# Attention and two MLPs on one core: the first four units' probabilities turned by a product with diagonals of reciprocals

## The chip, the cores and the metric

The kernel runs on one core of one Trainium2 chip. A core has TensorE (PE in the profile, its weight loads PEld), VectorE (DVE), ScalarE (ACT), GpSimd (POOL) and SyncE (SP, which here issues nearly all DMAs). The metric is device time in microseconds. The kernel before took 1039.23 us (median of three runs, 1036.81 to 1042.94).

## The reference

Inputs are q, k, v of shape (4, 8, 576, 64), s of shape (4, 8, 576), and two pairs of MLP weights, 512 x 2048 and 2048 x 512 in 64-bit floats.

```python
scores = scale * np.matmul(q, k.transpose(0, 1, 3, 2))
cum = np.cumsum(np.maximum(s, 0.0), axis=-1)
bias = -(cum[:, :, :, None] - cum[:, :, None, :])
scores = np.where(causal, -1e9, scores + np.minimum(bias, 0.0))
attn = np.exp(scores - max(scores))
attn = attn / (sum(attn) + 1e-09)
x = (attn @ v)                         # to 2304 x 512
x = (s1 * relu(x @ w_in1)**2 + b1) @ w_out1
h = x @ w_in2
out = (relu(h) + alpha * min(h, 0)) @ w_out2
```

## The kernel before, in words

Attention is cut into 32 units: a batch, a pair of heads, and a range of query rows. `units` (L272) lists them so that the first four units (n = 0 to 3) are batch 0, rows 0 to 319, its four pairs of heads. Each unit has two heads (h = 0, 1), and a head of these units has three blocks of query rows (`IB`, L52: 64, 128 and 128 rows).

For a head `scores` (L402) first writes the bias into the tile `probs`, from a running sum that a DMA has spread over the partitions (`u.cums`): on VectorE for head 0 (L433), on ScalarE for head 1 (L429). GpSimd masks it (L437). TensorE makes scores (L455), VectorE joins both and takes the maximum (L459), ScalarE takes the exponential and its row sums (L471). Then VectorE adds 1e-9 to the sums (L478) and takes their reciprocals (L479), and GpSimd multiplies each block of probabilities by them (L482, three instructions for a head of units 0 to 3).

`values` (L488) turns the probabilities on TensorE against `ident` (L513: six transposes of 128 x 128 for such a head, five into one PSUM bank and one into another). The banks are copied to SBUF by ScalarE and VectorE (L517), multiplied with v (L529), and copied into the rows of x (L544). `busy` (L94) issues products of a tile of zeros that nobody reads, on TensorE, in the first four units.

The running sums are made once (`sum_gates`, L109), written to `cum_d` in DRAM, and read back by `load_cum` (L345), two DMAs for a unit, each spread over 128 partitions. `load_qk` and `load_v` load q, k and v. `fetch(0, f)` (L189) loads packet f of the first MLP's weights, two DMAs of 512 KB, and `packet(0, f)` turns it into pairs of 32-bit tiles: ScalarE L140 and L130, VectorE L141, L142 and L131, GpSimd L131 for half of it. The order of these loads at the start is written out in `attention` (L565 to L586). Tiles of units 1 to 3 lie in slots of the weights to come, which `early_bufs` hands out in the order of the calls.

The first MLP block starts when all four units of batch 0, rows 0 to 319, are in x (`while done < reached(0)`, L978). Behind that TensorE works through 128-row products of the two MLPs with the other attention units in between (`pace`, L965). The order in which the instructions stand in each engine's queue is planned ahead for the whole program, from the order of the program text and from modelled costs; on the chip each engine then takes its queue strictly in that order, and a wait holds all that stands behind it.

The slopes of the second MLP (`nalpha`) are loaded by `load_constants` in the opening (L104, a DMA of single elements of 4 bytes, and L105 on VectorE); they are first read in the second MLP (L826), from 642.7 us on.

Of the kernel before, what the change touches and what calls it, by code (L numbers as in the profile page):

```python
# [8 lines left out]
F32 = mybir.dt.float32  # L9
# [4 lines left out]
ALU = mybir.AluOpType  # L14
# [5 lines left out]
def tile_forget_attention__then__two_mlps(  # L20
# [20 lines left out]
    nc = tc.nc  # L41
    B, H, S, D = q.shape
    NT, DM = out.shape
    DFF = w_in1.shape[1] // 2
    P = 128
    NP = H // 2
    NCC = DM // P
    NF = DFF // P
# [3 lines left out]
    IB = [(0, 64)] + [(64 + 128 * n, 192 + 128 * n) for n in range(4)]  # L52
    R1 = IB[2][1]
    QK = S - R1 + S
    EARLY, NATIVE = NP, 2 * NP

# [3 lines left out]
    REBASE, W_SCALE = 2.0**-111, 2.0**8  # L62
# [4 lines left out]
    one = ctx.enter_context(tc.tile_pool(name="one", bufs=1))  # L67
# [33 lines left out]
    def load_constants():  # L101
        nc.sync.dma_start(out=gate_s, in_=act_s.partition_broadcast(P))
        nc.sync.dma_start(out=gate_b, in_=act_b.partition_broadcast(P))
        nc.sync.dma_start(out=nalpha, in_=alpha.rearrange("(f p) -> p f", p=P))  # L104
        nc.vector.tensor_scalar(out=nalpha, in0=nalpha, scalar1=-1.0, scalar2=None, op0=ALU.mult)  # L105
        nc.vector.tensor_scalar(out=gate_s, in0=gate_s, scalar1=1.0 / W_SCALE, scalar2=None, op0=ALU.mult)
        nc.vector.tensor_scalar(out=gate_b, in0=gate_b, scalar1=1.0 / W_SCALE, scalar2=None, op0=ALU.mult)

    def sum_gates(first):  # L109

# [165 lines left out]
    class Unit:  # L276
        def __init__(self, n):
            self.n = n
            self.b, self.pr, self.rng = units[n]
            self.tag = "_".join(str(i) for i in units[n])  # L280
            self.h0 = 2 * self.pr
            self.blocks = (0, 1, 2) if self.rng == 0 else (3, 4)
            self.q0, self.q1 = (0, R1) if self.rng == 0 else (R1, S)
            self.nv = 3 if self.rng == 0 else 4
            self.probs = [None, None]

            self.early = 0 < n < EARLY
            self.native = n < NATIVE
            self.n_banks = 0
            self.cums = []  # L290

# [53 lines left out]
    def load_cum(u, heads=(0, 1)):  # L345
        for h in heads:
            cr = u.buf(two, S, F32, "cum", f"cum{h}")
            (nc.sync if u.n else nc.scalar).dma_start(
                out=cr[:, : u.q1], in_=cum_d[u.b * H + u.h0 + h, : u.q1].partition_broadcast(P)
            )  # L350
            u.cums.append(cr)
# [50 lines left out]
    def scores(u, h):  # L402
# [11 lines left out]
        for r in u.blocks:  # L414
            i0, i1 = IB[r]
            rows = i1 - i0
            if u.early and r != 1:
                big, col = u.buf(two, 0, F32, "", f"probs{h}{r}"), 0

            width = -(-i1 // P) * P if i1 < S else S  # L420
            pt = probs[r] = big[:, col : col + width]
            col += width
            if width > i1:
                nc.gpsimd.memset(pt[:, i1:], 0.0)
            if r == 0:
                nc.gpsimd.memset(pt[64:P, 0:64], 0.0)

            if flip:
                nc.scalar.activation(  # L429
                    pt[:rows, :i1], u.cums[h][:rows, :i1], AF.Relu, scale=-1.0, bias=cumT[:rows, r, head : head + 1]  # L430
                )
            else:
                nc.vector.tensor_scalar(  # L433
                    out=pt[:rows, :i1], in0=u.cums[h][:rows, :i1], scalar1=cumT[:rows, r, head : head + 1],
                    scalar2=0.0, op0=ALU.subtract, op1=ALU.min,
                )
            nc.gpsimd.affine_select(  # L437
                out=pt[:rows, i0:i1], in_=pt[:rows, i0:i1], pattern=[[-1, rows]], base=0,
                channel_multiplier=1, compare_op=ALU.is_ge,
                fill=-MASKED if flip else MASKED,  # L440
            )
# [35 lines left out]
            busy(4)  # L477
        nc.vector.tensor_scalar(out=sm[:, :nr], in0=sm[:, :nr], scalar1=1e-9, scalar2=None, op0=ALU.add)  # L478
        nc.vector.reciprocal(sm[:, :nr], sm[:, :nr])  # L479
        for m, r in enumerate(u.blocks):  # L480
            rows, n = IB[r][1] - IB[r][0], IB[r][1]
            nc.gpsimd.tensor_scalar(  # L482
                out=probs[r][:rows, :n], in0=probs[r][:rows, :n], scalar1=sm[:rows, m : m + 1],
                scalar2=1.0, op0=ALU.mult, op1=ALU.mult,
            )
        yield

    def values(u, h):  # L488
# [10 lines left out]
        for n_bank, bank in enumerate(banks):  # L499
            f0, fn = bank[0][1], bank[-1][1] + width[bank[-1][0]]  # L500
            tp = u.bank("tr", f"pt{h}_{n_bank}")
            moves = []
            for c, off in bank:
                for r in u.blocks:
                    i0, i1 = IB[r]
                    if P * c >= i1:
                        continue

                    partial = r and P * c > i0
                    o = off + i0 - max(q0, P * c)  # L510
                    moves.append((not partial, -c if partial else o, o, r, min(P * c, S - P)))
            for _, _, o, r, k0 in sorted(moves):
                nc.tensor.transpose(tp[:, o : o + P], u.probs[h][r][:, k0 : k0 + P], ident)  # L513
            n_p = (2 * h + n_bank) % 2
            if u.native:
                pf = two.tile([P, 512], F32, tag=("ph", "pl")[n_p], name=f"pf_{u.tag}_{h}_{n_bank}")
                (nc.scalar.copy, nc.vector.tensor_copy)[n_p](pf[:, f0:fn], tp[:, f0:fn])  # L517
                parts = (pf,)
            else:
                ph = two.tile([P, 512], F32R, tag="ph", name=f"ph_{u.tag}_{h}_{n_bank}")  # L520
                pl = two.tile([P, 512], F32R, tag="pl", name=f"pl_{u.tag}_{h}_{n_bank}")
                split(ph[:, f0:fn], pl[:, f0:fn], tp[:, f0:fn])
                parts = (ph, pl)
            yield
            for z, part in enumerate(parts):
                for c, o in bank:
                    w = width[c]
                    lhs = (u.vn if u.native else u.vs[h])[:, c].rearrange("p z d -> p (z d)")
                    nc.tensor.matmul(  # L529
                        av[:, nq - w : nq], lhs, part[:, o : o + w],  # L530
                        start=(c == 0 and z == 0), stop=(c == last_c and z == len(parts) - 1),
                        skip_group_check=True,
                    )
# [28 lines left out]
    def attention():  # L562
# [5 lines left out]
        load_qk(us[2])  # L568
        load_v(us[0])
        load_cum(us[1])  # L570
        fetch(0, 0)
        load_qk(us[3])
        load_cum(us[2])
        load_v(us[1])
        packet(0, 0)
        load_cum(us[3])
        fetch(0, 1)
        load_v(us[2])
        load_v(us[3])
# [13 lines left out]
        u = Unit(EARLY)  # L593
# [391 lines left out]
    for n in range(len(BLOCKS) * NF):  # L985
# [13 lines left out]
            lent.clear()  # L999
        if n == NF - 2:  # L1000
            sum_columns()
        if len(late) > LAG[layer]:
            step(*late.pop(0))

# [49 lines left out]
```

## Time and profile before

| | |
|---|---|
| median of three runs | 1039.23 us |
| profiled execution, its own time | 1039.36 us |
| its span (first to last instruction) | 1037.6 us |
| around the span | 1.8 us |
| PE busy | 1018.5 us (98%) |
| PEld busy | 925.5 us (89%) |
| DVE busy | 674.4 us (65%) |
| ACT busy | 670.7 us (65%) |
| POOL busy | 450.6 us (43%) |
| mean granted TensorE clock | 0.996 |

Busy time is what an engine spent in instructions; matmuls are pipelined and their ends are modelled, so a busy TensorE isn't one at its peak, and the share of weight loads (PEld) says more on that. A row of the timeline has start, duration, engine, line, operation, output and input, shape and count, and in brackets the idle time before it and what ended it. Rows with a count join several instructions and name the first one's shape. The granted clock is a share of 2.4 GHz.

### The profile page before, as it was taken

What the parts mean: (1) busy time and instruction counts of PE and PEld (TensorE: products, weight loads), DVE (VectorE), ACT (ScalarE), POOL (GpSimd) and SP (SyncE); (2) the same over time, 40 slices, a digit from 0 to 9 for tenths busy, and PEclk for the clock granted to TensorE, in tenths of its full rate; (3) what the DMA queues carried; (4) which work ended last, traced back from release to release, by engine and by line L of the source; (5) the groups of instructions that cost most, each with busy time, mean ns of one, the idle gap of its engine ahead of it and who ended that gap; (6) DMA issues with size and microseconds to landing.
All of it is one profiled execution on the core that took longest, in us unless ns stands there. A gap on an engine that the chain in (4) does not pass through costs nothing. (4 is left out here: it accounts for less than half of the span.)

```text
span 1037.6 us, 20643 instructions
## 1 busy us (share of the span) xinstructions
PE 1018.5 (98%) x6949; PEld 925.5 (89%) x6952; DVE 674.4 (65%) x1605; ACT 670.7 (65%) x1668; POOL 450.6 (43%) x876
## 2 busy tenths in 40 slices
PE   9999999999999999999999999999999999999997
PEld 4578899999999999999999888888999999999996
DVE  6899665687677766677655865857665456455443
ACT  5878766777787877878776776645554454445433
POOL 5555675666677576777562000574611011001000
PEclk9899999999999999999999999999999999999999
DMA  7997443343143432324215762645644335334331
GB/s 150 257 249 223 120 76 68 73 98 76 40 89 67 99 72 52 82 65 91 68 34 177 230 199 78 205 148 176 200 154 142 102 114 171 103 102 133 105 102 48
DMA packets 197930, 125.45 MB, mean 121 GB/s; under 512 B 138496, under 2 KB 167936, under 8 KB 197824
## 3 DMA queue, kind: packets, MB, share of 16 engines
q1 hardware_dynamic: 193744, 123.56, 42.8%
q8 instruction: 55, 0.90, 0.4%
q10 hardware_dynamic: 4080, 0.57, 0.3%
q14 instruction: 51, 0.42, 0.1%
HBM read 106.19 MB, written 17.90 MB: 120 GB/s over the span
## 5 line engine op out<-in xcount | busy, mean ns | idle before, releaser
L781 PE MATMUL hp<-xh,w 128*128 128x256 f32 (+1 forms) x1024 | 229.9, 301 | 1.1 <-ACT r L800 1.1
L905 PE MATMUL acc<-w,ring 128*128 128x512 f32 x864 | 214.6, 392 | 1.1 <-DVE ring L131 0.7
L905 PEld LDWEIGHTS acc<-w,ring 128*128 128x128 f32 x864 | 155.9, 188 | 29.4 <-DVE ring L131 1.1
L781 PEld LDWEIGHTS hp<-xh,w 128*128 128x128 f32 x1024 | 171.4, 189 | 9.3 <-ACT r L800 1.4
L895 PE MATMUL acc<-gh,w 128*128 128x256 f32 x896 | 170.3, 286 | 0.4 <-ACT res L924 0.4
L781 PE MATMUL hp<-xl,w 128*128 128x256 f32 (+1 forms) x512 | 152.3, 298 | 0.0
L895 PEld LDWEIGHTS acc<-gh,w 128*128 128x128 f32 x896 | 135.3, 189 | 2.4 <-ACT res L924 1.0
L881 POOL TENSOR_TENSOR cc<-u,t 128x256 f32<-128x256 f32 x32 | 26.9, 839 | 237.2 <-DVE u L872 202.9
L895 PE MATMUL acc<-gl,w 128*128 128x256 f32 x448 | 117.7, 288 | 1.4 <-POOL gl L131 1.4
L482 POOL TENSOR_SCALAR probs<-probs,sm 64x64 f32<-64x64 f32 (+4 forms) x160 | 89.2, 571 | 58.9 <-DVE sm L479 51.9
L471 ACT ACTIVATE probs<-probs,nm 64x64 f32<-64x64 f32 (+4 forms) x160 | 89.9, 562 | 35.8 <-DVE nm L459 26.9
L131 POOL TENSOR_TENSOR gl<-r,gh 128x256 fp32r<-128x256 f32 x112 | 87.7, 784 | 51.3 <-ACT gh L130 41.4
L815 PE MATMUL p<-xs,sums 128*128 128x256 f32 x768 | 104.6, 282 | 0.4 <-DVE u L857 0.4
L815 PEld LDWEIGHTS p<-xs,sums 128*128 128x128 f32 x768 | 98.0, 189 | 2.0 <-DVE u L857 0.6
L781 PEld LDWEIGHTS hp<-xl,w 128*128 128x128 f32 x512 | 97.1, 190 | 2.7
L459 DVE CUSTOM_DVE_ANT_0 probs<-sc,probs 128x320 f32<-128x320 f32 (+3 forms) x160 | 68.4, 428 | 42.1 <-PE sc L458 28.8
L815 PEld LDWEIGHTS p<-xs,w 128*128 128x128 f32 x576 | 79.0, 189 | 8.4 <-DVE u L872 1.7
L800 ACT ACTIVATE r<-hp 128x256 f32<-128x256 f32 (+1 forms) x144 | 58.0, 403 | 43.7 <-PE hp L781 31.6
L815 PE MATMUL p<-xs,w 128*128 128x256 f32 x576 | 82.0, 282 | 2.3 <-DVE u L872 1.5
L895 PEld LDWEIGHTS acc<-gl,w 128*128 128x128 f32 x448 | 79.8, 189 | 2.5 <-POOL gl L131 1.9
L513 PE MATMUL pt<-ident,probs 128*128 128x128 f32 x480 | 75.3, 275 | 3.1 <-POOL probs L482 2.7
L826 DVE SCALAR_TENSOR_TENSOR ph<-pl,misc,ph 128x512 f32<-128x512 f32 x64 | 50.6, 790 | 42.3 <-ACT pl L842 42.3
(151 smaller groups left out, 2104.3 us busy)
## 6 DMA issues: line engine op xcount, KB each, us to landing
sums<-sums_d SPq DMA_DIRECT2D x128, 256.0 KB, 2.7
wi<-in_moe_w_in_dram SPq DMA_DIRECT2D x32, 512.0 KB, 5.0
wo<-in_moe_w_out_dram SPq DMA_DIRECT2D x32, 512.0 KB, 5.1
cum<-cum_d SPq DMA_DIRECT2D x32, 288.0 KB, 3.6
sums_d<-w SPq DMA_DIRECT2D x64, 128.0 KB, 1.9
cum<-cum_d SPq DMA_DIRECT2D x30, 160.0 KB, 3.0
nat<-in_k_dram SPq DMA_DIRECT2D x64, 72.0 KB, 2.5
x_d<-res SPq DMA_DIRECT2D x18, 256.0 KB, 2.4
```

The source lines that it names most:

```text
L131: lo_eng.tensor_tensor(out=lo, in0=src, in1=hi.bitcast(F32), op=ALU.subtract)
L459: nc.vector.tensor_tensor_reduce(out=pt[:rows, j0:j1], in0=scr, in1=pt[:rows, j0:j1], scale=SCALE if flip else -SCALE, scalar=init, op0=AL ...
L471: nc.scalar.activation(pt[:rows, :n], pt[:rows, :n], AF.Exp, bias=nm[:rows, m : m + 1], scale=1.0 if flip else -1.0, accum_out=sm[:rows, m ...
L482: nc.gpsimd.tensor_scalar(out=probs[r][:rows, :n], in0=probs[r][:rows, :n], scalar1=sm[:rows, m : m + 1], scalar2=1.0, op0=ALU.mult, op1=A ...
L513: nc.tensor.transpose(tp[:, o : o + P], u.probs[h][r][:, k0 : k0 + P], ident)
L781: nc.tensor.matmul(hs, a[:, c], b[c], start=(n == 0), stop=(n == len(terms) * NCC - 1))
L800: relus.append(nc.scalar.activation(r, hs, AF.Relu, scale=1.0 / W_SCALE).ins)
L815: nc.tensor.matmul(bank, lhs[:, c * P : (c + 1) * P], rhs[:, c], start=(start and c == 0 and z == 0), stop=(c == 1 and z == 2), skip_group ...
L826: nc.vector.scalar_tensor_tensor(out=r, in0=u, scalar=nalpha[:, f : f + 1], in1=r, op0=ALU.mult, op1=ALU.add).ins
L881: nc.gpsimd.tensor_tensor(out=cc[:, T:], in0=u3, in1=t5, op=ALU.add)
L895: nc.tensor.matmul(banks[d] if count == 2 else acc[d // 2][:, d % 2], a[:, d * P : (d + 1) * P], b, start=(f == 0 and (d % 2 == 0 or count ...
L905: nc.tensor.matmul(banks[m], a[:, m * P : (m + 1) * P], b, start=(f == 0 and b is woh and a is gh), stop=(f == NF - 1 and a is gl),)
```

## The change

For units 0 to 3 (`SPREAD = 4`) GpSimd no longer multiplies the probabilities by the reciprocals. VectorE writes three diagonal matrices for a head (identity times reciprocal: 64 x 64, 128 x 128, 128 x 128) into a tile that shares its place with `xs0` or `xs1`, one place for each h; and the six transposes of a head become six ordinary 32-bit products with these diagonals, 64 or 128 columns wide, so that turning and scaling are one step. The zeroing of a quarter of the first block's tile (L426) falls away for these units.

The running sums of units 2 and 3 are asked for right behind those of unit 1, ahead of the first packet of weights. The slopes of the second MLP are loaded at the start of the third block of the first MLP (`n == 2 * NF`) and no longer in the opening.

```diff
-    EARLY, NATIVE = NP, 2 * NP
+    EARLY, NATIVE, SPREAD = NP, 2 * NP, 4
...
     def load_constants():
         nc.sync.dma_start(out=gate_s, in_=act_s.partition_broadcast(P))
         nc.sync.dma_start(out=gate_b, in_=act_b.partition_broadcast(P))
+        nc.vector.tensor_scalar(out=gate_s, in0=gate_s, scalar1=1.0 / W_SCALE, scalar2=None, op0=ALU.mult)
+        nc.vector.tensor_scalar(out=gate_b, in0=gate_b, scalar1=1.0 / W_SCALE, scalar2=None, op0=ALU.mult)
+
+    def load_slopes():
         nc.sync.dma_start(out=nalpha, in_=alpha.rearrange("(f p) -> p f", p=P))
         nc.vector.tensor_scalar(out=nalpha, in0=nalpha, scalar1=-1.0, scalar2=None, op0=ALU.mult)
-        nc.vector.tensor_scalar(out=gate_s, in0=gate_s, scalar1=1.0 / W_SCALE, scalar2=None, op0=ALU.mult)
-        nc.vector.tensor_scalar(out=gate_b, in0=gate_b, scalar1=1.0 / W_SCALE, scalar2=None, op0=ALU.mult)
...
+            self.spread = n < SPREAD
+            self.diag = [None, None]
...
-            if r == 0:
+            if r == 0 and not u.spread:
                 nc.gpsimd.memset(pt[64:P, 0:64], 0.0)
...
         nc.vector.reciprocal(sm[:, :nr], sm[:, :nr])
+        if u.spread:
+            u.diag[h] = one.tile([P, QK], F32, tag=f"xs{h}", name=f"diag{h}_{u.tag}")
         for m, r in enumerate(u.blocks):
             rows, n = IB[r][1] - IB[r][0], IB[r][1]
+            if u.spread:
+                turn = u.diag[h][:rows, m * P : m * P + rows]
+                nc.vector.tensor_scalar(
+                    out=turn, in0=ident[:rows, :rows], scalar1=sm[:rows, m : m + 1], scalar2=None, op0=ALU.mult
+                )
+                continue
             nc.gpsimd.tensor_scalar(
...
-                    moves.append((not partial, -c if partial else o, o, r, min(P * c, S - P)))
-            for _, _, o, r, k0 in sorted(moves):
+                    moves.append((not partial, -c if partial else o, o, r, min(P * c, S - P), max(0, P * c - i0)))
+            for _, _, o, r, k0, skip in sorted(moves):
+                if u.spread:
+                    rows = IB[r][1] - IB[r][0]
+                    at = (r - u.blocks[0]) * P
+                    nc.tensor.matmul(
+                        tp[:, o + skip : o + rows], u.probs[h][r][:rows, k0 : k0 + P],
+                        u.diag[h][:rows, at + skip : at + rows], start=True, stop=True,
+                    )
+                    continue
                 nc.tensor.transpose(tp[:, o : o + P], u.probs[h][r][:, k0 : k0 + P], ident)
...
         load_cum(us[1])
+        load_cum(us[2])
+        load_cum(us[3])
         fetch(0, 0)
         load_qk(us[3])
-        load_cum(us[2])
         load_v(us[1])
         packet(0, 0)
-        load_cum(us[3])
         fetch(0, 1)
...
+        if n == 2 * NF:
+            load_slopes()
```

## Rows read from the trace of the kernel before

**Rows 1.** Busy time of each engine by stretch, with granted clock and DMA share.
```profile
core 0: us, PE busy (x) PEld busy (x) DVE busy (x) ACT busy (x) POOL busy (x), PEclk, DMA share, GB/s
15.00:30.00 15.00, 13.72 (x61) 7.63 (x61) 11.62 (x45) 9.80 (x31) 9.68 (x29) 1.00 0.78 207
30.00:45.00 15.00, 13.70 (x53) 8.31 (x53) 11.85 (x47) 14.14 (x42) 5.84 (x14) 0.77 0.92 240
...
100.00:110.00 10.00, 10.00 (x66) 8.47 (x65) 9.98 (x22) 9.47 (x23) 7.48 (x12) 1.00 0.62 168
...
300.00:400.00 100.00, 100.00 (x836) 99.76 (x835) 71.36 (x207) 78.53 (x210) 67.91 (x141) 1.00 0.35 77
```

**Rows 2.** Idle time by what ended it, first 66 us: total us, times, longest.
```profile
PEld pt L513 <- POOL probs L482: 5.1, 8, 1.4
ACT probs L429 <- DMA cum<-cum_d: 4.5, 3, 2.0
...
DVE pf L517 <- PE pt L513: 2.7, 2, 1.3
...
DVE wt L141 <- ACT wt L140: 1.9, 2, 1.2
```

**Rows 3.** Groups by line and shape, first 60 us: GpSimd's multiplications.
```profile
L482 POOL TENSOR_SCALAR probs<-probs,sm 128x320 f32<-128x320 f32 x8 | 4.7, 588 | 0.0
...
L482 POOL TENSOR_SCALAR probs<-probs,sm 128x192 f32<-128x192 f32 x8 | 4.0, 495 | 0.0
...
L482 POOL TENSOR_SCALAR probs<-probs,sm 64x64 f32<-64x64 f32 x8 | 3.0, 381 | 14.0 <-DVE sm L479 7.9 <-DVE nm L468 5.9 <-DVE pf L517 0.2
```

**Rows 4.** Timeline of VectorE in the opening.
```profile
13.76 0.98 DVE L433 TENSOR_SCALAR probs<-cum,cumT 64x64 f32<-64x64 f32 x3 [0.61 <-DMA cum<-cum_d]
...
22.79 1.65 DVE L433 TENSOR_SCALAR probs<-cum,cumT 64x64 f32<-64x64 f32 x3
...
26.10 2.69 DVE L433 TENSOR_SCALAR probs<-cum,cumT 64x64 f32<-64x64 f32 x3
...
36.17 0.91 DVE L141 TENSOR_SCALAR wt<-wt 128x512 uint32<-128x512 uint32 x1
...
39.82 0.42 DVE L141 TENSOR_SCALAR wt<-wt 128x512 uint32<-128x512 uint32 x1
...
41.62 0.17 DVE L105 TENSOR_SCALAR misc<-misc 128x16 f32<-128x16 f32 x1
...
41.84 0.40 DVE L131 TENSOR_TENSOR xl<-xf,xh 128x256 fp32r<-128x256 f32 x1
...
48.06 0.68 DVE L131 TENSOR_TENSOR xl<-xf,xh 128x256 fp32r<-128x256 f32 x1
...
53.03 1.14 DVE L131 TENSOR_TENSOR xl<-xf,xh 128x256 fp32r<-128x256 f32 x1
```

**Rows 5.** Timeline of GpSimd: the half of a weight packet.
```profile
27.35 1.26 POOL L131 TENSOR_TENSOR w<-wt,w 128x512 fp32r<-128x512 f32 x1
```

**Rows 6.** Timeline of TensorE: one head's transposes, one head's products with v.
```profile
15.90 0.82 PE L513 MATMUL pt<-ident,probs 128*128 128x128 f32 x6
...
18.91 1.30 PE L529 MATMUL acc_first<-pf,vn 128*128 128x320 f32 x6
```

**Rows 7.** Timeline of SyncE: the running sums of units 2 and 3.
```profile
19.41 0.93 SPq L348 DMA_DIRECT2D cum<-cum_d  x2
...
21.39 0.96 SPq L348 DMA_DIRECT2D cum<-cum_d  x2
```

**Rows 8.** Busy time by stretch, single microseconds around the lower clock; columns as Rows 1.
```profile
33.00:34.00 1.00, 0.70 (x5) 0.50 (x6) 0.86 (x2) 0.97 (x5) 0.94 (x3) 1.00 0.96 353
...
36.00:37.00 1.00, 0.65 (x3) 0.50 (x3) 1.00 (x3) 1.00 (x5) 0.94 (x4) 0.57 0.99 320
...
42.00:43.00 1.00, 1.00 (x4) 0.38 (x2) 0.23 (x1) 0.97 (x3) 0.98 (x3) 0.52 1.09 416
```

## The prediction
> **What bounds the kernel now.** I read busy time by stretch first. Late in the kernel TensorE is the bound without doubt: from 300 to 400 us it is busy for 100.00 us of 100 and its weight loads for 99.76. In the opening it is not: its weight loads fill 7.63 of 15 us (15 to 30) and 8.31 of 15 (30 to 45), and much of what it does there is products of zeros. The fullest queues there are VectorE's, 11.62 and 11.85 of 15, with ScalarE's at 14.14 in the second of the two. VectorE stays full long into the first MLP block, 9.98 of 10 us from 100 to 110, with TensorE's weight loads at 8.47 [rows 1]. So the change, which touches the first 60 us and one small load later, is priced along VectorE's queue: what leaves it, what enters it, and which of its waits go. A microsecond won there is taken as one won at the end, because TensorE has no idle time behind.
>
> The view of waits says what the opening waits for: the weight loads of the transposes stood 5.1 us in all for GpSimd's multiplications (8 times), ScalarE 4.5 us for running sums that had not landed (3 times), VectorE 2.7 us for turned probabilities (twice) and 1.9 us for ScalarE's step of a weight packet (twice) [rows 2].
>
> **Part 1a: GpSimd's multiplications go.** Their three shapes took 4.7, 4.0 and 3.0 us, 11.7 us in all for the eight heads [rows 3]. GpSimd isn't the bound, so this is worth nothing by itself. It is worth something where an instruction of VectorE ran beside one and was longer for it. In VectorE's timeline I look for equal instructions with and without a multiplication beside them: a bias of three blocks took 1.65 us against 0.98; a 512-column shift 0.91 against 0.42 (two such); two low halves of x 0.68 and 1.14 against 0.40 [rows 4]. The excess is 0.67 + 2 x 0.49 + 0.28 + 0.74 = 2.7 us. Taken: -2.7. Bounds: 0, if GpSimd's other work moves into the same places, and -2.7.
>
> **Part 1b: VectorE gets 24 diagonals.** No row shows a 128 x 128 of this kind. The nearest are the same operation from SBUF to SBUF on 16 columns, 0.17 us, and on 512 columns, 0.42 us [rows 4]; between them 0.5 ns a column, so 0.19 us for 64 columns and 0.23 us for 128, 0.65 us for a head, 5.2 us for eight. Below, 24 x 0.17 = 4.1 us; above, a diagonal may meet a GpSimd instruction, which is a rival below. Not all of it is on the path: VectorE is idle for 3.4 + 3.15 = 6.5 us between 15 and 45 us [rows 1], of which 1.9 us goes by part 2, so 4.6 us of holes remain, some of them right behind a reciprocal, where it waits for the turned block. I let these hide 2.0 us. Taken: +3.2; bounds 0.6 (all holes used) and 5.2.
>
> **Part 1c: transposes become products.** A head's six transposes take 0.82 us. Six 32-bit products of 64 or 128 columns are two passes each, 2 x 576 = 1152 columns in all, which is just what a head's products with v have: 1.30 us [rows 6]. So TensorE gets 8 x 0.48 = 3.8 us more; the 12 weight loads in place of 6 could make it 6 to 8 us. Against that stand its waits for GpSimd, 5.1 us [rows 2], which shrink to the wait for one diagonal, some 0.3 us a head, 2.4 us. The time from reciprocal to turned block stays about as it was. Taken: 0, bounds -2.7 and +4. What hides it is VectorE's longer queue; without that cover it costs 3.8 us.
>
> **The clock.** From 36 to 43 us the granted clock is 0.57, then 0.50, then 0.52, the 1.2 GHz level (seven rows, first and last shown). Ahead of the fall TensorE had holes: busy 0.70 of the microsecond from 33, behind a wait for GpSimd [rows 8]. The level lasted some 6.1 us, 3 us of TensorE's time at full speed. With those waits shorter and more work in their place I expect less of it, hardly surely. On VectorE's queue it is worth one wait for turned probabilities, 1.3 us, the longer of the two [rows 2]. Taken: -1.3; bounds -3.0 and 0 (the lower clock stays, or comes elsewhere).
>
> **Part 2: running sums of units 2 and 3 earlier.** SyncE issued them at 19.41 and 21.39 us [rows 7]; right behind unit 1's they go out some 9 us earlier. ScalarE's two long waits for them, 3.9 of the 4.5 us, should go; on VectorE they came through as the 1.9 us in which it waited for ScalarE's step of a packet [rows 2]. Taken: -1.9; bounds -3.9 and 0. Moved behind them are the first packet of weights, unit 3's q and k and unit 1's v, each by two issues of 0.93 and 0.96 us [rows 7] and the 640 KB that they move. The first packet is used when the first MLP block starts, 35 us after it was ready, which hides 2 to 3 us. If ScalarE's first step on it stands in the queue ahead of an exponential, it costs up to those 3 us; I take 0.
>
> **Part 3: the slopes later.** One VectorE instruction of 0.17 us [rows 4] and one small DMA leave the opening; 200 us on, they meet a VectorE that is busy 71% of the time from 300 to 400 us [rows 1] and values not read before the second MLP. Taken: -0.2. If the load is slow to land, what stands behind the sign change on VectorE waits, at most for some microseconds, with TensorE's queue still full ahead of it; taken 0, above +2.
>
> **The sum.** -2.7 + 3.2 + 0 - 1.3 - 1.9 - 0.2 = -2.9 us. The profiled execution took 1039.36 us (span 1037.6 and 1.8 around it), 0.13 us over the median of the runs. 1039.36 - 2.9 = 1036.5 us. What a measurement here can tell from no change is about 0.5%, 5.2 us, so the likeliest case is no change by that measure.
>
> **Rivals.**
>
> Rival A, the opening hangs on TensorE more than on VectorE. For it: its waits for GpSimd are the longest of those that the change aims at, and the slow clock lies behind them. Against it: half of its work there is zeros. Then 5.1 (waits) + 3.0 (clock) + 1.9 (sums) - 3.8 (longer products) = 6.2 us go: 1033.1 us. It needs the lower clock to go wholly.
>
> Rival B, slower: the diagonals meet GpSimd's other instructions. The place is VectorE's queue between 27 and 50 us, beside the low halves of weight packets on GpSimd, 1.26 us each [rows 5]. The row of three biases at 26.10 us took 2.69 us in place of 0.98, beside that very instruction [rows 4]: 1.7 us lost. Then the diagonals cost their full 5.2 us, 4 of the 8 heads lose 1.26 us each, 5.0 us, nothing is won by 1a (GpSimd's weight halves move up into the places that came free), and the lower clock stays: 5.2 + 5.0 - 1.9 - 0.2 = +8.1, 1047.5 us. With two heads caught it is already +5.6. Against it: such blocks hit three or four instructions of VectorE now, among over a hundred. The Trainium skill, page "SBUF — State Buffer", section "Who interferes with whom", puts it as an exclusive lock: whichever of a VectorE instruction of this kind and a GpSimd instruction starts first has the shared ports for the whole instruction, and the other is fully blocked. By that rule a diagonal could lose a whole GpSimd instruction, and the rows just named agree with it, 2.69 against 0.98 us.
>
> Rival C, only VectorE's total counts. VectorE is full until 110 us [rows 1], and the opening's shorter waits only make it wait in the first MLP block for weights. Then +5.2 - 2.7 - 0.2 = +2.3 us: 1041.7 us.
>
> Rival D, the change does not do all it says: the order in the queues is planned for the whole program, and the moved sums, planned as landing in time either way, may stay where ScalarE waits. Then the sum lacks 1.9: 1038.4 us.
>
> **Chances.** The forecast 0.35, rival A 0.30, B 0.13, C 0.15, D 0.07. Faster by over 0.5% (under 1034.0) is most of A and a little of the forecast's own spread, 0.31; slower by over 0.5% (over 1044.6) is B and a little of C, 0.14; the rest, 0.55, lies within. The range runs from 1031.0 (A with the bound of 3.9 for the sums) to 1043.5 (C with up to 2 us of the slopes' load); below and above I leave 0.1 each. The likeliest case's own range is 1034 to 1039.
>
> **What would show it.** Right: ScalarE's waits for running sums down to that of unit 1; no excess on VectorE beside a multiplication; diagonals of about 0.2 us; six products of a head in 1.2 to 1.8 us; the first product of the MLP, now at 58.7 us, some 3 us earlier, and the rest of the kernel moved by as much. Wrong: diagonals of 1 us or more (B); the first MLP block starting earlier but ending no earlier (C); the granted clock never under 1.00 in the opening and a start more than 5 us earlier (A).

## The result: 0.9% slower, and the profile after

The changed kernel took 1048.3 us (median of six runs, 1043.36 to 1051.23) against 1038.83 for the kernel before (six runs, 1036.81 to 1042.94): ratio 1.0086, 95% interval 1.0066 to 1.0106. That is 9.5 us slower; 1036.5 was forecast, and 1048.3 lies over the top of the range. The profiled execution took 1047.07 us, its span is 1045.3 us and its mean granted clock 0.991 (before 1037.6 us and 0.996). In all that follows, a run that took over 1.5% more than the fastest of its kernel is left out of medians and ratios: three runs of e18 and one of the kernel before.

The page of the kernel after: busy time of TensorE, and its clock in 40 slices of 26 us.

```profile
PE 1030.1 (99%) x7000; PEld 936.2 (90%) x7000; DVE 670.3 (64%) x1629; ACT 673.6 (64%) x1668; POOL 438.9 (42%) x844
...
PEclk9699999999999999999999999999999999999999
```

TensorE is busy for 11.6 us more than before, more than the whole loss, and the second slice is the only one with a low clock. So the loss lies in the opening. Busy time by stretch of the kernel after, to be held against [rows 1]; the last row is the stretch at the 1.2 GHz level:

```profile
15.00:30.00 15.00, 14.27 (x73) 9.47 (x72) 10.25 (x48) 9.91 (x32) 5.67 (x22) 1.00 0.89 224
30.00:45.00 15.00, 13.23 (x44) 8.75 (x43) 11.03 (x40) 11.30 (x31) 3.23 (x6) 0.63 0.80 221
...
34.00:51.00 17.00, 16.98 (x49) 11.67 (x50) 10.26 (x38) 10.39 (x30) 2.58 (x4) 0.50 0.81 205
```

VectorE, the queue by which everything was priced, is now less busy in the opening than before, and TensorE is busy for 16.98 us of the 17 at the low clock. Who waits for whom has turned round. The view of waits of the kernel after, first 66 us, for ScalarE and VectorE:

```profile
ACT pf L537 <- PE pt L528: 8.6, 6, 3.3
ACT wt L142 <- DMA wi<-in_moe_w_in_dram: 1.5, 1, 1.5
ACT wt L142 <- DMA wo<-in_moe_w_out_dram: 1.2, 1, 1.2
...
DVE probs L463 <- PE sc L459: 7.3, 7, 2.2
DVE pf L537 <- PE pt L528: 4.0, 4, 1.5
DVE wt L143 <- ACT wt L142: 2.5, 2, 1.9
...
DVE turnedq L377 <- DMA natq<-in_q_dram: 0.4, 1, 0.4
```

The waits at which the change aimed are gone: none of ScalarE's for running sums and none of TensorE's for GpSimd's multiplications is left of [rows 2]. In their place ScalarE (8.6 us) and VectorE (7.3 and 4.0 us) wait for TensorE, and three loads are waited for that were not in the kernel before: the two of the second weight packet, and unit 3's q. VectorE's wait for ScalarE's step of a packet, which was to go, grew from 1.9 to 2.5 us.

What these waits lead to is seen in the timeline of the kernel after. First TensorE with a head's products at 2.4 GHz (12 instructions: each 32-bit product is two), then its two holes and products at 1.2 GHz; then SyncE's issues, ScalarE and VectorE ahead of the second hole.

```profile
16.54 1.78 PE L528 MATMUL pt<-diag,probs 128*128 128x64 f32 x12
23.56 1.80 PE L528 MATMUL pt<-diag,probs 128*128 128x64 f32 x12 [0.73 <-DVE diag L490]
34.02 1.00 PE L459 MATMUL sc<-turnedk,turnedq 64*128 64x192 f32 x2 [1.76 <-DVE nm L463]
38.42 2.72 PE L528 MATMUL pt<-diag,probs 128*128 128x64 f32 x10
...
9.94 2.81 SPq L352 DMA_DIRECT2D cum<-cum_d  x6
13.82 3.21 SPq L329 DMA_DIRECT2D natq<-in_q_dram  x4
17.08 4.90 SPq L329 DMA_DIRECT2D natk<-in_k_dram  x4
23.06 0.49 SPq L210 DMA_DIRECT2D wi<-in_moe_w_in_dram  x1
...
27.82 0.68 ACT L142 ACTIVATE wt<-wi 128x512 f32<-128x512 f32 x1 [1.48 <-DMA wi<-in_moe_w_in_dram]
30.22 0.67 ACT L142 ACTIVATE wt<-wo 128x512 f32<-128x512 f32 x1 [1.22 <-DMA wo<-in_moe_w_out_dram]
...
22.46 0.51 DVE L377 STREAM_TRANSPOSE turnedq<-natq 128x320 f32<-128x320 f32 x1 [0.41 <-DMA natq<-in_q_dram]
30.92 0.43 DVE L143 TENSOR_SCALAR wt<-wt 128x512 uint32<-128x512 uint32 x1 [1.91 <-ACT wt L142]
33.61 0.35 DVE L463 CUSTOM_DVE_ANT_0 probs<-sc,probs 128x192 f32<-128x192 f32 x1
```

Read from below: TensorE stood 1.76 us for a maximum of VectorE's, which stood behind weight work that had waited 1.91 us for ScalarE, which had waited 1.48 and 1.22 us for the second packet, issued from 23 us on. Behind that hole the granted clock is 0.50 for 17 us. The first product of the MLP starts at 71.99 us, before at 58.68 us; not all of these 13.3 us are lost, since more of the attention is done by then.

The second packet itself hardly moved. The kernel before issued it at 22.39 us, 0.67 us sooner, and ScalarE came to it only at 29.93 us, behind its waits for running sums, and found it there (SyncE and ScalarE of the kernel before):

```profile
22.39 0.44 SPq L208 DMA_DIRECT2D wi<-in_moe_w_in_dram  x1
29.93 0.67 ACT L140 ACTIVATE wt<-wi 128x512 f32<-128x512 f32 x1
```

Freed from those 3.9 us, ScalarE is there at 26.3 us in the kernel after, and stands 2.7 us for the packet instead.

**Where the time went.** The span is TensorE's idle time, plus what the low clock cost (busy time times one minus the granted clock, summed over stretches of 1 us), plus the rest, called its work at full clock. The work is worked out as this rest, so the three add up to the span in every row, whatever the cause:

| profiled execution | span | idle | lost to clock | work |
|---|---|---|---|---|
| before | 1037.6 | 19.1 | 3.3 | 1015.2 |
| after | 1045.3 | 15.2 | 8.5 | 1021.6 |

So work grew by 6.4 us, the clock cost 5.3 us more, and 3.9 us of holes went: 6.4 + 5.3 - 3.9 = 7.8 us, against 7.7 between the spans.

### The profile page after: what moved, and what is told of

It reads as the page before. It is cut to its first block, busy times and chain, and to the rows that moved or that the text cites. A ratio compares the mean times of both kernels' runs of the same rounds, so it can differ in the third digit from the quotient of the medians.

```text
span 1045.3 us, 20718 instructions
## 1 busy us (share of the span) xinstructions
PE 1030.1 (99%) x7000; PEld 936.2 (90%) x7000; DVE 670.3 (64%) x1629; ACT 673.6 (64%) x1668; POOL 438.9 (42%) x844
## 5 line engine op out<-in xcount | busy, mean ns | idle before, releaser
L915 PE MATMUL acc<-gh,w 128*128 128x256 f32 x896 | 172.4, 286 | 0.3 <-ACT res L944 0.3
L494 POOL TENSOR_SCALAR probs<-probs,sm 128x448 f32<-128x448 f32 (+4 forms) x136 | 77.8, 585 | 52.4 <-DVE sm L483 37.5
L567 DVE TENSOR_TENSOR xf<-av,xf 64x128 f32<-64x128 f32 (+3 forms) x88 | 28.1, 319 | 72.9 <-ACT xf L566 72.6
```

Of the source, the lines that this page charges most:

```text
L494: nc.gpsimd.tensor_scalar(out=probs[r][:rows, :n], in0=probs[r][:rows, :n], scalar1=sm[:rows, m : m + 1], scalar2=1.0, op0=ALU.mult, op1=A ...
L567: nc.vector.tensor_tensor(out=dst, in0=src, in1=dst, op=ALU.add)
L915: nc.tensor.matmul(banks[d] if count == 2 else acc[d // 2][:, d % 2], a[:, d * P : (d + 1) * P], b, start=(f == 0 and (d % 2 == 0 or count ...
```

## The experiments

Each ratio is to runs of the kernel before on the same chip (medians there 1037.8 to 1038.7 us). Clock is the median of the runs' mean granted clocks (kernel before: 0.996); idle, lost and work are those of the one profiled execution, which need not be like the median run: that of e4 is the longest of its twelve (1044.7 us), that of e2 one of two at a clock of 0.999.

| run | median us | ratio (95%) | clock | idle | lost | work |
|---|---|---|---|---|---|---|
| e1 sums, slopes | 1040.6 | 1.0012 (0.9999 to 1.0025) | 0.992 | 18.4 | 7.5 | 1014.1 |
| e2 products | 1040.4 | 1.0021 (1.0007 to 1.0034) | 0.996 | 15.8 | 0.0 | 1022.8 |
| e3 sums | 1038.5 | 1.0002 (0.9985 to 1.0019) | 0.993 | 16.3 | 6.2 | 1014.4 |
| e4 transposes twice | 1039.8 | 1.0011 (0.9994 to 1.0029) | 0.998 | 16.6 | 5.1 | 1021.3 |
| e5 more zeros | 1044.4 | 1.0060 (1.0036 to 1.0084) | 0.996 | 14.8 | 3.4 | 1024.1 |
| e6 twice, sums, slopes | 1040.2 | 1.0027 (1.0008 to 1.0046) | 0.996 | 15.3 | 5.1 | 1019.5 |
| e7 diagonals on GpSimd | 1041.2 | 1.0024 (1.0003 to 1.0045) | 0.997 | 15.6 | 0.0 | 1022.4 |
| e8 products, slopes | 1045.9 | 1.0068 (1.0053 to 1.0083) | 0.991 | 15.5 | 5.1 | 1022.8 |
| e9 products, sums | 1052.4 | 1.0109 (1.0072 to 1.0147) | 0.986 | 17.9 | 14.9 | 1019.5 |
| e10 slopes | 1040.4 | 1.0018 (1.0006 to 1.0030) | 0.996 | 18.7 | 4.8 | 1015.5 |
| e11 sums, zeros | 1038.7 | 0.9997 (0.9982 to 1.0012) | 0.998 | 16.1 | 5.0 | 1016.6 |
| e12 all, packet earlier | 1042.3 | 1.0054 (1.0032 to 1.0076) | 0.994 | 15.3 | 4.9 | 1020.7 |
| e13 sums, packet earlier | 1039.6 | 1.0011 (0.9995 to 1.0026) | 0.995 | 17.1 | 4.6 | 1015.5 |
| e14 products, sums, q and k first | 1035.7 | 0.9981 (0.9960 to 1.0002) | 1.000 | 13.3 | 0.0 | 1020.8 |
| e15 products, sums, packet earlier | 1043.5 | 1.0047 (1.0029 to 1.0065) | 0.994 | 15.6 | 6.6 | 1019.9 |
| e16 sums, q and k first | 1039.9 | 1.0012 (1.0001 to 1.0024) | 0.995 | 18.5 | 4.4 | 1013.4 |
| e17 all, q and k first | 1036.0 | 0.9977 (0.9967 to 0.9987) | 1.000 | 13.6 | 0.0 | 1021.0 |
| e18 products, sums, q and k in between | 1048.2 | 1.0062 (1.0023 to 1.0101) | 0.991 | 17.1 | 8.3 | 1021.0 |

### Parts alone, and the work without the change

```diff
# e1: the kernel after without products
-SPREAD = NP, 2 * NP, 4
+SPREAD = NP, 2 * NP, 0
# e2: the kernel after, load_cum and load_slopes in their old places
# e3: the kernel before, load_cum as in the kernel after
# e4: the kernel before
-nc.tensor.transpose(...)
+for _ in range(2 if u.n < 4 else 1): nc.tensor.transpose(...)
```

> The changed kernel without its products (units 0 to 3 turned and scaled as before), with the sums early and the slopes late. Theory T1 (the products load TensorE, 1.78 us a head in place of 0.82, and the opening then hangs on TensorE and its lower clock): 1036 to 1039 us, first MLP product near 58 us. Theory T2 (the first weights, moved back, come late; ScalarE, VectorE and TensorE wait for them in turn, and the clock falls): still 1044 to 1048 us, with a hole on TensorE near 33 us. Theory T3 (VectorE's 24 diagonals, 7.0 us, fill its queue): 1036 to 1039 us.

> The kernel before with the products alone; sums and slopes stay where they were. T1: 1044 to 1048 us, most or all of the loss, first MLP product 66 to 72 us. T2: 1037 to 1040 us. T3: 1044 to 1048 us, with VectorE full and TensorE waiting for diagonals.

> The kernel before with the early sums alone. T1 and T3: 1036 to 1039 us, ScalarE's 3.9 us of waits for sums gone. T2: 1044 to 1048 us, ScalarE waiting for weights near 28 and 30 us.

> The kernel before, with every transpose of units 0 to 3 issued twice into the same place: 48 more on TensorE, some 6.6 us at 0.14 us each, nothing more on any other engine. T1: 1042 to 1046 us, slower by about the added time. T2 and T3 (TensorE has room in the opening): 1038 to 1040 us.

No part alone costs more than 0.2%, together they cost 0.9%: the loss is not in a part. The column of work goes by the products: with them, or with transposes twice, 1019.5 to 1024.1 us, without 1013.4 to 1016.6. By a head's 1.78 us less the 0.82 of [rows 6] it should be 0.96 x 8 = 7.7 us more; against the 1015.2 us of the kernel before it is 4.3 to 7.6 us in the kernels with products (e5 with its added zeros aside). What varies more, from 0 to 14.9 us, is the clock. The sums alone already open a hole: in the profile of e3 TensorE stands 2.36 us for GpSimd, and the clock falls in it (TensorE and a window of e3):

```profile
24.00 1.54 PE L513 MATMUL pt<-ident,probs 128*128 128x128 f32 x6 [2.36 <-POOL probs L482]
...
22.00:36.00 14.00, 11.99 (x32) 6.53 (x32) 10.52 (x34) 10.41 (x29) 7.70 (x17) 0.53 0.95 271
```

### Holes filled, work doubled, diagonals moved

```diff
# e5: the kernel after
-busy(1)
+busy(9 if (u.n, h, r) == (2, 0, 0) else 1)
# e6: e1 and e4 together (the kernel after, transposes twice in place of products)
# e7: the kernel after
-nc.vector.tensor_scalar(out=turn, ..., op0=ALU.mult)
+nc.gpsimd.tensor_scalar(out=turn, ..., scalar2=1.0, op0=ALU.mult, op1=ALU.mult)
# e8: the kernel after, load_cum in its old places
```

> The changed kernel with eight more products of zeros on TensorE behind the first scores of unit 2, head 0, near the hole of 1.76 us ahead of the fall of its clock; 8 x 0.22 = 1.8 us more work. Theory C (the loss is TensorE's longer work, 6.4 us, plus its lower clock, 5.3 us more than before, minus 3.9 us fewer holes): the clock stays up longer, 1041 to 1046 us. Theory I (the three parts only make the order planned for the queues worse, and the clock follows from it): 1047 to 1051 us, the added work on top.

> The changed kernel with transposes and GpSimd's multiplications as before in units 0 to 3, but every transpose issued twice: TensorE's load near that of the products without a diagonal on VectorE. Theory C: near the changed kernel, 1044 to 1049 us, as TensorE's work and the hole behind the moved weights are both there. Theory I or T3 (diagonals): near the kernel without products, 1040 to 1042 us.

> The changed kernel with its 24 diagonals made by GpSimd, 7.0 us off VectorE's queue. T3 (VectorE's diagonals are the loss): 1038 to 1041 us. Theory C: 1046 to 1050 us, unchanged.

> The changed kernel with the sums of units 2 and 3 back in their old places (products and late slopes stay). Theory C with the moved loads as the cause of the hole: no fall of the clock before 40 us, 1039 to 1042 us, like the products alone. If the slopes are what makes the difference: 1046 to 1050 us.

e5 took 1044.4 us: eight more products of zeros ahead of the hole at 32 us left none there, but TensorE now stood 1.98 us for a diagonal at 24 us, and the clock fell at 26 us instead. e6, as much work and as many waits of the old kind, stays at 1040.2 us (three of its twelve runs took 1045.6 to 1047.8): work alone is not the loss. e7 takes 7 us away, but its runs reach from 1037.8 us at a clock of 0.999 to 1050.5 at 0.982, so it did not tell the load on VectorE from the clock. e8 against e2 is the clearest view of how sharply the clock turns. Up to 40 us both have the same order in the queues of TensorE, ScalarE and VectorE; unit 3's sums land 0.55 us later in e8. ScalarE's wait and the windows, first e2, then e8:

```profile
27.70 1.15 ACT L434 ACTIVATE probs<-cum,cumT 64x64 f32<-64x64 f32 x3 [2.04 <-DMA cum<-cum_d]
...
28.00:30.00 2.00, 1.04 (x4) 0.71 (x5) 0.48 (x4) 2.00 (x6) 1.36 (x7) 1.00 1.15 341
30.00:34.00 4.00, 4.00 (x22) 2.38 (x20) 3.19 (x9) 3.17 (x9) 1.77 (x3) 1.00 1.00 292
```

```profile
28.25 1.15 ACT L433 ACTIVATE probs<-cum,cumT 64x64 f32<-64x64 f32 x3 [2.48 <-DMA cum<-cum_d]
...
28.00:30.00 2.00, 0.58 (x4) 0.39 (x3) 0.53 (x4) 1.75 (x5) 1.06 (x6) 1.00 1.05 391
30.00:34.00 4.00, 4.00 (x15) 2.90 (x15) 2.99 (x8) 3.79 (x10) 2.15 (x4) 0.57 1.17 313
```

TensorE is idle for 0.96 us of these two in e2 and the clock stays at 1.00; for 1.42 us in e8, and the next 4 us run at 0.57. This is the profiled execution of e2; ten of its twelve runs have a mean clock of 0.992 to 0.997, so in most of them the clock fell somewhere too, at about the same time of 1040 us. And e8 loses without a moved sum and without a wait for unit 3's q.

### Which moved load

```diff
# e9: the kernel after, load_slopes in its old place
# e10: the kernel before, load_slopes in its new place
# e11: e3
-busy(1)
+busy(9 if (u.n, h, r) == (1, 1, 1) else 1)
# e12: the kernel after
 fetch(0, 0)
+fetch(0, 1)
 load_qk(us[3])
 load_v(us[1])
 packet(0, 0)
-fetch(0, 1)
```

> The changed kernel with the slopes' load back in its old place: products and earlier sums remain. So far: products alone 1040.4, sums alone 1038.5, products with late slopes 1045.9, all three 1048.3. Theory L (the late slopes shift the planned order, and with the products' fuller TensorE queue that opens holes and the 1.2 GHz level follows): this kernel is near products alone, 1039 to 1042 us, with under 4 us lost to the clock. Theory M (the first weights, moved behind the sums, make ScalarE wait and open the hole by themselves): it stays at 1046 to 1049 us with the lower clock from about 34 us on.

> The kernel before with only the slopes' load moved to the second MLP block in program order. The prediction's part 3 gives -0.2 us: 1038.3. Theory L gives a loss that is smaller than with the products, +1 to +3 us (sums alone 1038.5, sums with late slopes 1040.6): 1039.5 to 1041.5, with TensorE's work unchanged at some 1014.6 us and the rest in the clock. If it is 1038 to 1039, the late slopes harm only together with another part.

> Sums alone, with eight more products of zeros behind unit 1's second scores of head 1, where TensorE waited 2.4 us (21.6 to 24.0) for the block multiplied on GpSimd and the granted clock was 0.50 from 22 to 36 us. If the wait is what the fall of the clock follows, the level stays at 1.00 there, 4 to 6 of the 6.24 us lost to the clock come back and the fillers cost nothing, since they stand in the hole: 1033 to 1035 us, under the kernel before. Rival: the fall only comes at the next hole (there was one of 2.65 us), and the time stays at 1037.5 to 1039.5.

> The changed kernel with the loads of the second weight packet issued right behind the first's, ahead of unit 3's q and k. In the changed kernel ScalarE waited 1.48 and 1.22 us for them, VectorE 1.91 us behind it, TensorE 1.76 us for VectorE at 32 to 34 us, and the clock fell for 17 us. If this chain is the cause, the waits go, 3 to 6 us of the 8.5 lost to the clock come back, and the time is 1042 to 1045 us: what is left over the kernel before is then the products. Rival: the planned order leaves another hole for the same reason (a fuller TensorE queue with the same fixed order) and the time stays at 1046 to 1049 us.

My theory L, that the late slopes do the harm, falls with e9: without them the loss is still there (1.0109, with an interval that overlaps that of the whole change). Its profile shows the first hole at its plainest. VectorE, then TensorE, then two windows of e9:

```profile
23.31 0.51 DVE L378 STREAM_TRANSPOSE turnedq<-natq 128x320 f32<-128x320 f32 x1 [1.95 <-DMA natq<-in_q_dram]
...
23.83 0.63 DVE L491 TENSOR_SCALAR diag<-ident,sm 64x64 f32<-64x64 f32 x3
...
24.41 3.04 PE L529 MATMUL pt<-diag,probs 128*128 128x64 f32 x12 [2.26 <-DVE diag L491]
...
22.00:24.00 2.00, 0.15 (x1) 0.00 (x0) 0.69 (x5) 1.21 (x5) 0.00 (x0) 1.00 0.30 47
24.00:55.00 31.00, 29.76 (x87) 20.94 (x90) 17.61 (x67) 15.65 (x42) 4.99 (x9) 0.51 0.95 249
```

The reciprocal was there at 21.4 us (its row starts at 21.20). The diagonals made from it stand in VectorE's queue behind the turning of unit 3's q, and that waits 1.95 us for a load that the change had moved behind four running sums. TensorE is idle for 1.85 of 2 us, and then has its clock at 0.51 for 31 us. The kernel after has the same order on VectorE and TensorE up to 40 us, and waits 0.41 us there: the length differs from one execution to the next. The wait stands in the profiles of most kernels with both sums and first packet ahead of unit 3's q: 1.23 us in e1, 0.41 in e3, 1.67 in e5, 0.85 in e11; in e6, e7 and e13, and in those with the old order (before, e2, e8), it is not there. With it e1, which has no products, still takes 1040.6 us: the wait alone is not the loss.

e12 wins back 6 us (1042.3, though five of its twelve runs took 1044.8 to 1049.5), but it is not a clean test of the second packet alone: ScalarE's waits for that packet go, and in the new plan the diagonals also stand ahead of the turning of unit 3's q on VectorE. A hole of 1.35 us is left ahead of 34.94 us, and the clock is low for 11 us behind it (TensorE and a window of e12):

```profile
34.94 2.14 PE L528 MATMUL pt<-diag,probs 128*128 128x64 f32 x12 [1.35 <-DVE diag L490]
...
36.00:47.00 11.00, 10.53 (x36) 7.53 (x35) 5.42 (x22) 6.68 (x20) 2.20 (x2) 0.53 0.74 160
```

In its profile e11 kept the clock at 1.00 to 46 us, through a hole of 1.17 us at 23 us, and lost it behind another of 1.18 us at 43 us: no gain in the median. Five of its twelve runs had a clock of 0.999 or more, and took 1035.7 to 1036.3 us; that is the time of e14 and e17 below, without the products. A window of e11:

```profile
46.00:56.00 10.00, 9.74 (x25) 6.28 (x25) 7.63 (x23) 5.81 (x17) 5.70 (x13) 0.50 1.13 294
```

```diff
# e13: e3 with fetch(0, 1) as in e12
# e14: e9
 load_cum(us[1])
+load_qk(us[3])
 load_cum(us[2])
 load_cum(us[3])
 fetch(0, 0)
-load_qk(us[3])
# e15: e12 with load_slopes in its old place
```

> Sums alone, with the second packet's loads ahead of unit 3's q and k; no products, slopes in their old place. Sums alone took 1038.5 us with 6.24 us lost to the clock in its profile. If the late second packet is what opens the holes there too, 3 to 5 of them come back: 1033.5 to 1036 us, under the kernel before (some 1038.3). Rival: without products the fall of the clock at 22 us hangs on GpSimd's multiplications and on unit 3's q, which now lands later: 1038 to 1040 us.

> Products and sums (slopes in their old place), with unit 3's q and k issued ahead of the sums of units 2 and 3. Theory Q (VectorE's 1.95 us for unit 3's q, with the diagonals behind it in its fixed order, opens the hole of 2.26 us at 22 us and the clock falls behind it): that wait goes and the time falls from 1052.4 to 1040 to 1044 us. Rival (ScalarE's wait for the weight packets decides, and these come later still here): 1046 us or more.

> Products and sums with the second packet's loads ahead of unit 3's q and k, slopes in their old place. All three parts with that packet earlier took 1042.3 us. If the late slopes cost something of their own (sums with them 1040.6 against 1038.5, products with them 1045.9 against 1040.4), this is 1039 to 1041.5 us, near the products alone; if they do not, it is 1042 to 1044.

e14 is the test that decides. With unit 3's q and k three calls further up, products with sums go from 1052.4 to 1035.7 us, under the 1040 to 1044 that I had expected (two of its twelve runs still took 1044.2 and 1045.2, at clocks of 0.990 and 0.989). e15 (1043.5) against e12 (1042.3) shows no loss of the slopes' own, and e13 (1039.6) none of the gain hoped for without products.

### The change with one call moved

```diff
# e16: e3 with load_qk(us[3]) as in e14
# e17: the kernel after, whole, with load_qk(us[3]) as in e14
# e18: e9
 load_cum(us[1])
-load_cum(us[2])
-load_cum(us[3])
 fetch(0, 0)
 load_qk(us[3])
+load_cum(us[2])
+load_cum(us[3])
```

> The kernel before with the sums of units 2 and 3 ahead of the first weights and unit 3's q and k ahead of these sums; transposes, GpSimd's multiplications and the slopes as before. If products only load TensorE (some 7.8 us of work, of which holes gave back 3 to 4), this is below the same with products: 1031 to 1035 us. Rival: without them TensorE waits for GpSimd again, the clock falls behind such a hole, and the time is 1037 to 1040 us: then the products are worth it once the loads stand right.

> The changed kernel whole (products, earlier sums, late slopes) with only unit 3's q and k issued ahead of the moved sums. If VectorE's wait for unit 3's q is the cause of the loss of 9.5 us, it falls from 1048.3 to 1035 to 1040 us. Rival: the late slopes have a loss of their own (products with slopes were at 1045.9), and it stays at 1042 to 1046.

> Products and sums, slopes in their old place; the loads go first packet, unit 3's q and k, sums of units 2 and 3, unit 1's v: q and k as early as in the kernel before, the sums between their old and their new place. If the 2 us by which the moved sums delayed q and k are the cause of the loss (products with sums: 1052.4 us), the time falls to the level of products alone, 1038 to 1042 us. If what helped was that q and k came ahead of the 1 MB of the first packet (1035.7 us), it stays at 1044 us or more.

e17 is the whole change with that one call moved: 1036.0 us, all twelve runs within 1034.7 to 1036.9, 12.3 us under the kernel after and, at a ratio of 0.9977, under the kernel before as well. SyncE's issues, ScalarE, VectorE, TensorE and a window of e17, against the same of the kernel after:

```profile
11.22 1.94 SPq L329 DMA_DIRECT2D natq<-in_q_dram  x4
13.20 1.98 SPq L329 DMA_DIRECT2D natk<-in_k_dram  x4
15.23 1.88 SPq L352 DMA_DIRECT2D cum<-cum_d  x4
20.00 0.69 SPq L210 DMA_DIRECT2D wi<-in_moe_w_in_dram  x1
...
30.00 0.68 ACT L142 ACTIVATE wt<-wi 128x512 f32<-128x512 f32 x1
...
18.96 0.51 DVE L377 STREAM_TRANSPOSE turnedq<-natq 128x320 f32<-128x320 f32 x1 [0.30 <-DMA cum<-cum_d]
21.63 0.74 DVE L490 TENSOR_SCALAR diag<-ident,sm 64x64 f32<-64x64 f32 x3
...
22.32 1.80 PE L528 MATMUL pt<-diag,probs 128*128 128x64 f32 x12 [0.17 <-ACT probs L433]
...
34.00:51.00 17.00, 16.99 (x90) 12.09 (x90) 16.68 (x57) 15.43 (x41) 4.64 (x7) 1.00 0.87 213
```

SyncE's issues of k take 1.98 us in place of 4.90, because the first packet's 1 MB stands no longer ahead of them; so the second packet goes out 3 us earlier too, though its call was not moved. Both holes are gone, and from 34 to 51 us TensorE runs 90 instructions in place of 49 at the full clock. The first MLP product starts at 56.45 us.

The moved call changes more than the loads. The planned order of the queues is another one too: ScalarE's parts from that of the kernel after at 15.3 us, VectorE's at 17.2 us, TensorE's at 26.7 us, and ScalarE now takes its first step on the second packet at 30.00 us, when it has landed. So e14 and e17 show that the place of this one call decides; whether it is by q and k landing sooner, by the second packet going out sooner or by the new order, no run tells apart.

e16 shows what the products are worth then. Without them TensorE has no hole from 13 to 42 us; from there on it stands for the copies, for VectorE's sums of rows and for GpSimd again (TensorE of e16, the two longest), the clock falls, and the time is 1039.9 us:

```profile
48.32 2.27 PE L455 MATMUL sc<-turned 64*128 64x448 f32 x6 [1.87 <-DVE sm L478]
52.13 1.54 PE L513 MATMUL pt<-ident,probs 128*128 128x128 f32 x6 [1.53 <-POOL probs L482]
```

So the extra work of the products pays for itself here, by waits that it removes, where the loads stand as in e17. That it takes products is not shown: the five runs of e11 at full clock got there with products of zeros.

e18 goes against a simpler reading, that the 2 us by which the sums delayed q and k are the whole cause. With q and k as early as in the kernel before, VectorE has no wait for them, and TensorE still waits 1.38 us for a diagonal at 24 us, with the clock at 1.00 behind it. The profiled execution (1048.2 us) loses its clock later: TensorE stands 2.00 us for ScalarE, which had waited for the running sums of a later unit, and the clock is 0.50 from 51 to 67 us (TensorE, then ScalarE, of e18):

```profile
51.18 2.39 PE L550 MATMUL av<-pf,vn 128*128 128x320 f32 x6 [2.00 <-ACT pf L538]
...
49.32 1.33 ACT L434 ACTIVATE probs<-cum,cumT 128x448 f32<-128x448 f32 x2 [1.42 <-DMA cum<-cum_d]
```

Three of ten runs took 1038.2 to 1039.1 us at clocks of 0.998 and 0.999, the others 1048.2 us and more at 0.991 or less. The same kernel is at the level of the products alone where its clock holds, and 10 us over it where it does not. So a loss of this size needs no late q. In e14 and e17 q and k went ahead of the 1 MB too, not only of the sums, and that, or the order that came with it, is what helped.

## Why the prediction was wrong, step by step

**The step that failed** is part 2, with the clock behind it. Its first half took -1.9 us for VectorE's wait behind ScalarE. ScalarE's 3.9 us for the sums of units 2 and 3 did go, but it then stood 2.7 us for the second packet, and VectorE's wait behind it was 2.5 us in place of 1.9. Its second half says: "Moved behind them are the first packet of weights, unit 3's q and k and unit 1's v ... I take 0". It priced the first packet, and left q and k and the second packet without a price or a reader. The reader of q is VectorE, and part 1b put the diagonals into the same queue behind it. What ran in its place: a wait on VectorE for q (0.41 us in the profile after, with a hole of 0.73 us on TensorE and the clock still at 1.00; 1.95 us in that of e9, with a hole of 2.26 us and the clock falling), then ScalarE's for the second packet, a hole of 1.76 us, and the 1.2 GHz level for 17 us. With the one call for q and k moved, the rest of the change took 1036.0 us. Which link of this chain the moved call cuts stays open, as said above.

That 1036.0 us lies close to the 1036.5 of the forecast is luck. Against the kernel before, e17 has 5.8 us more work, 5.5 us less idle time and 3.3 us less lost to the clock, and the sum had been made up of VectorE's terms.

**What bounds the kernel.** Wrong in the opening: "a microsecond won there [on VectorE] is taken as one won at the end". VectorE got emptier (8.10 of 15 us busy from 45 to 60, before 13.98) and the kernel slower. TensorE's queue, with its holes and at the clock that it has, is the better measure: among the kernels with products, the lost clock time alone goes from 0.0 to 14.9 us, and the four slowest (e9, after, e18, e8) have the lowest clocks, 0.986 to 0.992.

**Part 1a.** The multiplications went as said, and no wait for them is left. The time does not show what VectorE won by it.

**Part 1b.** The rows of the kernel after: 16 of 128 x 128 took 286 ns each, 8 of 64 x 64 took 376 ns, 6.4 us busy in all, 5.2 forecast. One of eight heads met a GpSimd instruction (VectorE of the kernel after; its three diagonals took 1.67 us, those of other heads about 0.63):

```profile
33.89 1.27 DVE L490 TENSOR_SCALAR diag<-ident,sm 64x64 f32<-64x64 f32 x1
```

So rival B, whose time of 1047.5 us came nearest to the result, had the wrong reason: the meeting cost 1 us once, not 5 us. The lock that the Trainium skill describes (page "SBUF — State Buffer", section "Who interferes with whom") agrees with that row, as GpSimd's low half of a packet runs from 33.84 to 35.12 us beside it; it decides nothing here.

**Part 1c.** The size was wrong and so was the cover. Counting columns as in the products with v gave 0.48 us a head; it is 0.96, or 7.7 us in all, inside the "6 to 8" named for the weight loads, 12 in place of 6. "What hides it is VectorE's longer queue" did not hold: in the profiled execution work grew by 6.4 us and holes gave back 3.9, a net 2.5 us, inside the bound of +4.

**The clock.** Taken -1.3, it was +5.3 in the profiled execution, outside the bound of 0 that was named as "comes elsewhere" without a price. Over the runs, 0.992 in place of 0.996 is some 4 us of 1038, near half of the loss; an estimate from the two medians, and a rough one, as e2's runs at 0.995 and at 0.999 took the same 1040 us.

**Part 3.** Taken -0.2. Alone it cost +1.9 us (e10, 1.0018), and the slopes did not leave the opening: the order planned for the whole program has their DMA at 48.50 us, before at 33.30. In e17 they cost nothing (0.9977, with the slopes in their old place 0.9981 in e14). How a load at 48 us costs 1.9 us is not shown.

**Rivals.** A had the right engine, TensorE, with the wrong sign. C and D did not come: the loss is not 2.3 us, and ScalarE's waits for the sums did go. The ends of the range, 1031.0 and 1043.5, come out at 1031.1 and 1043.7 us from the terms that they name; nothing hangs on it.

**Still open:** why e8 is 5.5 us over e2 in every run. Its second low stretch (57 to 65 us, clock 0.57) has only a hole of 0.41 us close ahead of it, at 54 us; the two kernels' orders part on VectorE at 41 us and on ScalarE at 49 us, and no run tells which instruction does it. Also open is what brings the level down at 10 us in e4 and e6, where no hole stands ahead in the rows.

## What to carry to other kernels

When a load is moved behind others, price each load that now stands behind it: name the instruction that waits for it and everything queued behind that one, above all work that the same change has just put there. Where an engine is 98% busy, a hole of a microsecond or two on it is worth more than its length if the clock falls behind it; count a change as work, holes and clock, not as one queue's sum. When a wait is taken away from a queue, look at what the queue will reach sooner, and whether that is there yet. And before a change that loses is thrown away, undo its parts in pairs: no part alone showed this loss, and one call moved turned it into a gain.

## What the runs showed of the hardware

- A 32-bit product of a 128-row block with a 128 x 128 or 64 x 64 diagonal is two instructions; twelve took 1.78 us, where six transposes of the same blocks took 0.82 us [rows 6].
- The granted clock fell to 0.50 in or behind holes of 1.35 us (e12), 1.42 us (e8), 1.76 us (after) and 2.36 us (e3), and stayed there for some 11, 4, 17 and 14 us, although TensorE was busy nearly all the while. Behind holes of 1.25 us (e2, at 23 us), 1.39 us (e8, at 23 us) and 1.38 us (e18) it stayed at 1.00: the length of the hole alone does not settle it.
- The mean clocks of single runs of one kernel went from 0.984 to 0.999 (e18), with times from 1051 to 1038 us. So a comparison of this kernel to half a per cent needs the clock beside the time.
- Four issues of 40 KB each on SyncE took 4.90 us behind 1 MB of weights and 1.98 us ahead of it (behind it 5.08 in the kernel before and 4.76 in e18; ahead of it 1.97 in e14 and 1.98 in e16).
